# Attention in 64-row and 64x64 tiles of TensorE, with the keys split 64+8 a head

## The chip, the cores and the metric

One core of a Trainium2 chip runs the kernel. The metric is the device time of one execution in microseconds, as the median of the runs whose state is fast. A ratio is the mean time of one kernel's fast runs over that of the other's fast runs of the same rounds on the same chip, so it is not quite the ratio of the medians that stand beside it. The profile is of one execution; its span is 1 to 2 us shorter than the time.

## The reference

```python
# B, H, S, D = 8, 8, 576, 64 ; pool 8, so 72 pooled keys a head
k_p = k.reshape(B, H, 72, 8, D).mean(axis=3)
v_p = v.reshape(B, H, 72, 8, D).mean(axis=3)
a   = softmax(q @ k_p^T / sqrt(D))              # B, H, 576, 72
x   = (a @ v_p) -> (4608 tokens, 512)           # heads side by side
h   = x @ w_in                                  # 512 -> 2048
out = (h - tanh(h)) @ w_out                     # 2048 -> 512
```

## The kernel before

The kernel is one software pipeline. Tokens go through the MLP in nine groups of 512; between the MLP products of group g stands the attention of batch g+1. A score slot serves two heads. Their 2 x 72 = 144 pooled keys are too many for 128 partitions, so 128 of them go in one tile and 16 are left over. The 128 keys of a pair of heads fill all rows: the keys of the one head lie in rows 0 to 63 of the contraction, those of the other in 64 to 127, with zeros between. In AV a mask on the values keeps the heads apart.

```python
def score_mms(b, t, dst, c0, c1, pairs=range(NM)):      # two products of 288 columns a slot
    for m in pairs if t == NM else (t,):
        ...
        nc.tensor.matmul(dst[p : p + w], lhsT=KB[b % 2][:, o : o + w],
                         rhs=qTs[b][:, m, c0:c1], start=True, stop=True)

def av_half(b, blk, half, x_sb, alloc):                 # three products of 130 columns a half
    ...
    ps = alloc([128, 4, D1], FP32, "x_ps")
    for n in range(3):
        nc.tensor.matmul(..., lhsT=E[:, t, c0 : c0 + 128], rhs=vb[:, s0 : s0 + 2, :], ...)
```

All loads of batches 1 to 7 are issued by the sync engine (SP), in the order keys, values, queries. The same engine issues the stores of the output and the transposes by DMA (queries, keys, x). Each main load is one transfer of 128 rows:

```python
def load_main(src, dst, b, t0, t1):
    return nc.sync.dma_start(out=dst[:, t0:t1, :], in_=src[b, 0:128, t0:t1, :])
def load_v(b):
    return [load_main(v_pairs, v_raw[b % 2], b, 0, NM)] + load_left(v_pairs, v_raw[b % 2], b)
...
for g in range(1, NG):                                  # the loop over token groups
    for i in range(NHID):
        mlp_h(g, i, gts)
        if i == 0 and g > 1:
            pool_k(nb, nc.gpsimd); pool_v(nb, nc.gpsimd)
        if i == (3 if g == 1 else 8):
            k_dma_transpose(nb); k_place(nb, nc.gpsimd.tensor_copy)
            load_k(nb + 1); load_v(nb + 1); load_q(nb + 1)
```

The softmax here doesn't subtract the row's maximum and nothing guards it: scores larger than these inputs give would overflow.

Of the kernel before, what the change touches and what calls it, by code (L numbers as in the profile page):

```python
# [31 lines left out]
KP = 160  # L32
# [5 lines left out]
def kernel(  # L38
# [19 lines left out]
    ps_h = ctx.enter_context(tc.tile_pool(name="ps_h", bufs=3, space=PSUM))  # L58
    ps_o = ctx.enter_context(tc.tile_pool(name="ps_o", bufs=2, space=PSUM))
    ps_a = ctx.enter_context(tc.tile_pool(name="ps_a", bufs=3, space=PSUM))  # L60
# [14 lines left out]
    spread = const.tile([128, 128], BF16, name="spread")  # L75
    mask = const.tile([128, 3 * NM, 1], FP32, name="mask")
    k_raw = [const.tile([128, NT, POOL * D], FP32, name=f"k_raw{i}") for i in range(2)]
    v_raw = [const.tile([128, NT, POOL * D], FP32, name=f"v_raw{i}") for i in range(2)]
    KB = [const.tile([128, NM * KP], BF16, name=f"KB{i}") for i in range(2)]
    q_bf = const.tile([128, R + 1, H, D], BF16, name="q_bf")  # L80
    warm = const.tile([128, 1], FP32, name="warm")
    VB = [const.tile([128, 3 * NM, D1], BF16, name=f"VB{i}") for i in range(2)]
# [18 lines left out]
    def load_main(src, dst, b, t0, t1):  # L101
        return nc.sync.dma_start(out=dst[:, t0:t1, :], in_=src[b, 0:128, t0:t1, :])

    def load_left(src, dst, b, eng=nc.sync):
        return [
            eng.dma_start(out=dst[32 * t : 32 * t + LO, NM, :], in_=src[b, 128:PR, t, :])
            for t in range(NM)
        ]

    def load_dense(src, dst, b, eng=nc.sync):  # L110
        return eng.dma_start(
            out=dst[0 : NM * LO, NM, :], in_=src[b, 128:PR, :, :]
        )

    def load_k(b):
        return [
            load_main(k_pairs, k_raw[b % 2], b, 0, NM),
            load_dense(k_pairs, k_raw[b % 2], b),
        ]

    def load_v(b):
        return [load_main(v_pairs, v_raw[b % 2], b, 0, NM)] + load_left(
            v_pairs, v_raw[b % 2], b
        )
# [67 lines left out]
    def pool_k(b, eng, t0=0, t1=NT, mid=()):  # L192
        r = k_raw[b % 2].rearrange("p t (j d) -> p t j d", d=D)[:, t0:t1, :, :]
        if b not in kdups:
            kdups[b] = work.tile([128, NT, 2, D], BF16, name="kd", tag="kd")
        kd = kdups[b][:, t0:t1, :, :]
        n = t1 - t0
        first = eng.tensor_tensor(  # L198
            out=r[:, :, 0:4, :], in0=r[:, :, 0:4, :], in1=r[:, :, 4:8, :], op=ALU.add
        )  # L200
        for c in mid:
            load_w2(c)
        eng.tensor_tensor(  # L203
            out=r[:, :, 0:2, :], in0=r[:, :, 0:2, :], in1=r[:, :, 2:4, :], op=ALU.add
        )
        eng.tensor_tensor(  # L206
            out=kd,
            in0=r[:, :, 0:1, :].to_broadcast([128, n, 2, D]),
            in1=r[:, :, 1:2, :].to_broadcast([128, n, 2, D]),
            op=ALU.add,  # L210
        )
        return first

    def pool_v(b, eng):
# [8 lines left out]
            out=r[:, :, 0, :], in0=r[:, :, 0, :], in1=r[:, :, 1, :], op=ALU.add  # L223
        )
        v_main(VB[b % 2], r[:, :, 0:1, :], eng, 0, NM)
        v_left(VB[b % 2], r[:, NM, 0:1, :], eng)

    def v_main(vb, vs, eng, t0, t1):
        n = t1 - t0
        eng.tensor_tensor(  # L230
            out=vb[:, 2 * t0 : 2 * t1, 0:D].rearrange("p (t s) d -> p t s d", s=2),
            in0=vs[:, t0:t1, :, :].to_broadcast([128, n, 2, D]),
            in1=mask[:, 2 * t0 : 2 * t1, :]
            .rearrange("p (t s) o -> p t s o", s=2)
            .to_broadcast([128, n, 2, D]),
# [3 lines left out]
    def v_left(vb, vs, eng):  # L239
        eng.tensor_tensor(  # L240
            out=vb[:, 2 * NM :, 0:D],
            in0=vs.to_broadcast([128, NM, D]),
            in1=mask[:, 2 * NM :, :].to_broadcast([128, NM, D]),
            op=ALU.mult,
        )

    def kb_main(kb, ps, t0, t1, engs):
        kv = kb.rearrange("p (t x) -> p t x", x=KP)
        engs[0](out=kv[0:D, t0:t1, 0:G], in_=ps[0:D, :, 0:G])
        engs[1](out=kv[D:128, t0:t1, G:128], in_=ps[D:128, :, G:128])  # L250

    def kb_left(kb, ps, eng):
        eng(
            out=kb[D:128, :].rearrange("p (t x) -> p t x", x=KP)[:, :, 128 : 128 + LO],
            in_=ps[D:128, 0 : NM * LO].rearrange("p (x t) -> p t x", t=NM),
        )
# [10 lines left out]
    def k_transpose(b, alloc, engs=(nc.vector.tensor_copy, nc.scalar.copy)):  # L267
        kd = kdups.pop(b)
        ps = alloc([128, NM, 128], FP32, "kT_ps")
        for t in range(NM):  # L270
            turn_tile(ps[:, t, :], kd, t)
        kb_main(KB[b % 2], ps, 0, NM, engs)
        ps = alloc([128, 128], FP32, "kT_ps")
        turn_tile(ps[:, :], kd, NM)
        kb_left(KB[b % 2], ps, nc.vector.tensor_copy)

    kTs = {}

    def k_dma_transpose(b):
        kT = work.tile([128, NT, 128], BF16, name="kT", tag="kT", bufs=1)  # L280
        nc.sync.dma_start_transpose(
            out=kT[:, :, :], in_=kdups.pop(b)[:, :, :, :].rearrange("p t a d -> p (t a d)")
        )
        kTs[b] = kT

    def k_place(b, eng):
        kT = kTs.pop(b)
        kb_main(KB[b % 2], kT[:, 0:NM, :], 0, NM, (eng, eng))
        kb_left(KB[b % 2], kT[:, NM, :], eng)

    E_tiles = {}

    def score_mms(b, t, dst, c0, c1, pairs=range(NM)):
        for m in pairs if t == NM else (t,):
            o = m * KP + (128 if t == NM else 0)
            w = 32 if t == NM else 128
            p = 32 * m if t == NM else 0
            nc.tensor.matmul(  # L298
                dst[p : p + w],
                lhsT=KB[b % 2][:, o : o + w],  # L300
# [5 lines left out]
    def scores(b, t):  # L306
        if t == 0:
            E_tiles[b] = work.tile([128, NT, S], BF16, name="E", tag="E")
        E = E_tiles[b]
        hs = S // 2  # L310
        pss = []
        for half in range(2):
            ps = ps_a.tile([128, hs], FP32, name="s_ps", tag="ps_a")
            score_mms(b, t, ps[:, :], half * hs, (half + 1) * hs)
            pss.append(ps)
        for half, ps in enumerate(pss):
            nc.scalar.activation(  # L317
                out=E[:, t, half * hs : (half + 1) * hs], in_=ps[:, :], func=ACT.Exp, scale=SCALE
            )

    def scores_wide(b, ts):
        if b not in E_tiles:
            E_tiles[b] = work.tile([128, NT, S], BF16, name="E", tag="E")
        E = E_tiles[b]
        for t in ts:
            ps = ps_any([128, QA], FP32, "s_ps")
            score_mms(b, t, ps[:, :], 0, QA)
            nc.scalar.activation(out=E[:, t, 0:QA], in_=ps[:, :], func=ACT.Exp, scale=SCALE)

    def scores_tail(b):  # L330
        ps = ps_any([128, NT, QT], FP32, "s_ps")
        for t in range(NT):
            score_mms(b, t, ps[:, t, :], QA, S)
        nc.scalar.activation(
            out=E_tiles[b][:, :, QA:S], in_=ps[:, :, :], func=ACT.Exp, scale=SCALE
        )

    def av_half(b, blk, half, x_sb, alloc):
        E = E_tiles[b]
        vb = VB[b % 2]  # L340
        c0 = blk * 128 if blk < 4 else S - 128
        ps = alloc([128, 4, D1], FP32, "x_ps")
        for n in range(3):
            t = 2 * half + n if n < 2 else NM
            s0 = 2 * t if n < 2 else 2 * NM + 2 * half
            nc.tensor.matmul(  # L346
                ps[:, 2 * n : 2 * n + 2, :].rearrange("p h d -> p (h d)")
                if n < 2
                else ps.rearrange("p (a s) d -> p a s d", s=2)[:, :, 1, :],
                lhsT=E[:, t, c0 : c0 + 128],  # L350
                rhs=vb[:, s0 : s0 + 2, :].rearrange("p h d -> p (h d)")
                if n < 2
                else vb[:, s0 : s0 + 2, :],
                start=(n == 0),
                stop=(n == 2),
                skip_group_check=True,
            )
        rden = work.tile([128, 4, 1], FP32, name="rden", tag="rden", bufs=4)
        nc.vector.reciprocal(out=rden[:, :, :], in_=ps[:, :, D:D1])  # L359
        nc.vector.tensor_tensor(  # L360
            out=x_sb[:, half, :, :],
            in0=ps[:, :, 0:D],
            in1=rden[:, :, :].to_broadcast([128, 4, D]),
            op=ALU.mult,
        )

    def new_x():
        return work.tile([128, 2, 4, D], BF16, name="x_sb", tag="x_sb", bufs=4)

    def av(b, blk, alloc, by_dma):  # L370
        x_sb = new_x()
        for half in range(2):
            av_half(b, blk, half, x_sb, alloc)
        if by_dma:
# [4 lines left out]
                in_=x_sb[p0:128, :, :, :].rearrange("p a h d -> p (a h d)"),  # L379
# [3 lines left out]
    def x_pe_transpose(b, blk, x_sb, fbs=(0, 4)):  # L383
        p0 = 0 if blk < 4 else 64
        pos = b * S + blk * 128
        f0, f1 = fbs
        xf = x_sb.rearrange("p a h d -> p (a h d)")
# [417 lines left out]
```

## Time and profile before

| | before |
|---|---|
| time, median of fast runs | 301.04 us (300.99 to 301.22) |
| span of the profile | 299.1 us |
| TensorE busy, granted clock | 97%, 1.00 |
| one undisturbed token group with attention | 30.81 us |
| first tanh (the start is over) | 21.9 us |

The group times in this document are the distances between the first tanh of one token group and that of the next, read from ScalarE's rows in the trace. The chain (the work that ended last, followed back from each piece to what released it) is shown in the prediction. What matters for the argument and is not shown there is how the sync engine issues the loads of one batch. This is its time line in the kernel before (start in us, length in us, engine and line, operation, target and source, number of instructions):

```profile
126.53 0.57 SPq L102 DMA_DIRECT2D k_raw<-in_k_dram  x1
127.16 0.63 SPq L111 DMA_DIRECT2D k_raw<-in_k_dram  x1
127.84 0.58 SPq L102 DMA_DIRECT2D v_raw<-in_v_dram  x1
128.46 1.93 SPq L106 DMA_DIRECT2D v_raw<-in_v_dram  x4
130.44 0.42 SPq L135 DMA_DIRECT2D q_raw<-in_q_dram  x1
132.17 0.67 SPq L127 DMA_DIRECT2D q_raw<-in_q_dram  x1
```

An issue here takes about half a microsecond of the engine, for 1 MB (0.57 and 0.58) as for the small left-over transfers (0.63, and 1.93 for four), and the whole batch is issued in 6.3 us. After that the queue is free for stores and transposes.

### The profile page before, as it was taken

To read this page: it belongs to the slowest core of one execution; us is meant where nothing else is said; L and a number is where in the kernel's file an instruction comes from. 1 tells how busy PE (TensorE), PEld (TensorE's weight loads), DVE (VectorE), ACT (ScalarE), POOL (GpSimd) and SP (SyncE) were. 2 spreads that over 40 slices of the span, in tenths; PEclk is the share of its full clock that TensorE was granted. 3 is DMA by queue.
4 is the path that set the end of the run, shared out by engine and by line. 5 is a ranking of instruction groups with operands and counts; after the bars stand their busy time and mean duration, and the time that the engine had idled before them with its cause. 6 is when DMAs were issued, how large, how long until landed. Compare 5 with 4: busy or idle time off the path is not lost.

```text
span 299.1 us, 4694 instructions
## 1 busy us (share of the span) xinstructions
PE 291.5 (97%) x1671; PEld 142.5 (48%) x1671; DVE 159.1 (53%) x343; ACT 149.4 (50%) x283; POOL 115.5 (39%) x110
## 2 busy tenths in 40 slices
PE   7989999999999999999999999999999999999994
PEld 3454455544544454445444554455445544444443
DVE  5658665673547444753476247716680758108600
ACT  4647583666146633654265516650665166126511
POOL 8500904871496109922971089307940000000000
PEclk9999999999999999999999999999999999999999
DMA  7999999849854998699648974897431430111032
GB/s 251 226 211 278 311 227 310 263 87 328 234 113 99 271 297 134 117 302 245 107 88 235 300 167 94 242 294 159 97 66 35 95 92 0 37 70 36 0 72 70
DMA packets 66183, 49.79 MB, mean 166 GB/s; under 512 B 39920, under 2 KB 52976, under 8 KB 66160
## 3 DMA queue, kind: packets, MB, share of 16 engines
q1 hardware_dynamic: 58832, 42.94, 56.0%
q0 software_dynamic: 4752, 4.72, 9.4%
q10 hardware_dynamic: 2576, 1.84, 2.3%
q8 instruction: 13, 0.21, 0.3%
q14 instruction: 10, 0.08, 0.1%
HBM read 36.70 MB, written 9.44 MB: 154 GB/s over the span
## 4 chain that ended last, share of the span: by engine, by line
PE 85%; DMA 9%; POOL 4%; issue 0%; SPq 0%; ACT 0%; DVE 0%; POOLq 0%
PE o_ps L456 40%; PE hT_ps L428 37%; DMA w1b<-in_moe_w_in_dram 4%; PE x_ps L346 4%; DMA k_raw<-in_k_dram 4%; PE s_ps L298 3%; POOL k_raw L198 1%; DMA out_dram<-o_sb 1%; POOL k_raw L203 1%; POOL kd L206 1%; POOL w2b L510 0%; PE xT_ps L390 0%; POOL v_raw L576 0%; PE qT_ps L171 0%; POOL w1b L503 0%
## 5 line engine op out<-in xcount | busy, mean ns | idle before, releaser
L456 PE MATMUL o_ps<-w2b,gT 128*128 128x512 bf16 x560 | 134.4, 380 | 0.0
L441 DVE TENSOR_TENSOR gT<-hT_ps,t_sb 128x512 bf16<-128x512 f32 x144 | 98.9, 691 | 57.7 <-ACT t_sb L439 57.6
L428 PE MATMUL hT_ps<-xT,w1b 128*128 128x512 bf16 x576 | 126.9, 379 | 0.3 <-ACT xT L397 0.3
L439 ACT ACTIVATE t_sb<-hT_ps 128x512 f32<-128x512 f32 x144 | 85.6, 597 | 38.3 <-PE hT_ps L428 37.5
L428 PEld LDWEIGHTS <-w1b 128*128 128x128 bf16 x576 | 55.9, 98 | 66.5 <-issue 0.4
L456 PEld LDWEIGHTS <-gT 128*128 128x128 bf16 x560 | 52.5, 98 | 52.0 <-issue 1.4
L465 ACT COPY o_sb<-o_ps 128x512 f32<-128x512 f32 x33 | 19.3, 585 | 75.2 <-PE o_ps L456 75.2
L359 DVE RECIPROCAL rden<-x_ps 128x4 f32<-128x4 f32 x80 | 14.2, 177 | 52.5 <-PE x_ps L346 52.0
L360 DVE TENSOR_TENSOR x_sb<-x_ps,rden 128x256 bf16<-128x256 f32 x80 | 34.0, 425 | 3.5 <-DMA xT<-x_sb 0.6
L148 POOL CAST q_bf<-q_raw 128x2048 bf16<-128x2048 f32 x6 | 11.3, 1888 | 59.9 <-issue 34.8
L198 POOL TENSOR_TENSOR k_raw<-k_raw 128x1280 f32<-128x1280 f32 x7 | 20.2, 2886 | 27.4 <-DMA k_raw<-in_k_dram 16.6
L317 ACT ACTIVATE E<-s_ps 128x288 bf16<-128x288 f32 x60 | 21.4, 410 | 13.2 <-PE s_ps L298 13.0
L346 PE MATMUL x_ps<-VB,E 128*128 128x130 bf16 x240 | 20.8, 221 | 0.4 <-ACT xT L397 0.3
L346 PEld LDWEIGHTS <-E 128*128 128x128 bf16 x240 | 16.9, 98 | 8.8 <-DVE VB L230 0.6
L216 POOL TENSOR_TENSOR v_raw<-v_raw 128x1280 f32<-128x1280 f32 x6 | 17.4, 2898 | 0.0
L298 PE MATMUL s_ps<-qT,KB 128*128 128x288 bf16 (+5 forms) x128 | 17.0, 290 | 0.2
L298 PEld LDWEIGHTS <-KB 128*128 128x128 bf16 (+1 forms) x128 | 7.0, 96 | 10.2 <-issue 3.5
L527 PE MATMUL warm_ps<-xT 128*128 128x512 bf16 x29 | 10.2, 465 | 1.3 <-DVE xT L539 1.3
L206 POOL TENSOR_TENSOR kd<-k_raw 128x640 bf16<-128x640 f32 x7 | 10.8, 1540 | 0.5
L203 POOL TENSOR_TENSOR k_raw<-k_raw 128x640 f32<-128x640 f32 x7 | 10.8, 1541 | 0.5
L397 ACT CAST xT<-xT_ps 128x256 bf16<-128x256 f32 (+1 forms) x14 | 5.8, 436 | 8.5 <-PE xT_ps L390 5.1
L219 POOL TENSOR_TENSOR v_raw<-v_raw 128x640 f32<-128x640 f32 x6 | 9.3, 1544 | 0.5
(73 smaller groups left out, 100.7 us busy)
## 6 DMA issues: line engine op xcount, KB each, us to landing
k_raw<-in_k_dram SPq DMA_DIRECT2D x7, 1024.0 KB, 5.9
q_raw<-in_q_dram SPq DMA_DIRECT2D x7, 1024.0 KB, 10.2
v_raw<-in_v_dram SPq DMA_DIRECT2D x7, 1024.0 KB, 9.3
out_dram<-o_sb SPq DMA_DIRECT2D x38, 128.0 KB, 2.4
out_dram<-o_sb SPq DMA_DIRECT2D x16, 256.0 KB, 3.7
w1b<-in_moe_w_in_dram POOLq DMA_DIRECT2D x4, 512.0 KB, 14.2
w2b<-in_moe_w_out_dram POOLq DMA_DIRECT2D x4, 512.0 KB, 16.9
k_raw<-in_k_dram SPq DMA_DIRECT2D x7, 128.0 KB, 5.8
```

The source lines that it names most:

```text
L198: first = eng.tensor_tensor(out=r[:, :, 0:4, :], in0=r[:, :, 0:4, :], in1=r[:, :, 4:8, :], op=ALU.add)
L216: eng.tensor_tensor(out=r[:, :, 0:4, :], in0=r[:, :, 0:4, :], in1=r[:, :, 4:8, :], op=ALU.add)
L298: nc.tensor.matmul(dst[p : p + w], lhsT=KB[b % 2][:, o : o + w], rhs=qTs[b][:, m, c0:c1], start=True, stop=True,)
L317: nc.scalar.activation(out=E[:, t, half * hs : (half + 1) * hs], in_=ps[:, :], func=ACT.Exp, scale=SCALE)
L346: nc.tensor.matmul(ps[:, 2 * n : 2 * n + 2, :].rearrange("p h d -> p (h d)") if n < 2 else ps.rearrange("p (a s) d -> p a s d", s=2)[:, :, ...
L359: nc.vector.reciprocal(out=rden[:, :, :], in_=ps[:, :, D:D1])
L360: nc.vector.tensor_tensor(out=x_sb[:, half, :, :], in0=ps[:, :, 0:D], in1=rden[:, :, :].to_broadcast([128, 4, D]), op=ALU.mult,)
L428: nc.tensor.matmul(h_tiles[i][:, :], lhsT=w1b[:, fb, i * 128 : (i + 1) * 128], rhs=xT[:, fb, tok0 : tok0 + TG], start=(fb == 0), stop=(fb ...
L439: nc.scalar.activation(out=t_sb[:, :], in_=h_ps[:, :], func=ACT.Tanh)
L441: nc.vector.tensor_sub(out=gT[:, :], in0=h_ps[:, :], in1=t_sb[:, :])
L456: nc.tensor.matmul(o_ps[:, :], lhsT=gts[i][:, tb * 128 : (tb + 1) * 128], rhs=w2b[:, i, :], start=(i == 0), stop=(i == NHID - 1),)
L465: (nc.vector.tensor_copy if g == 0 and tb % 2 else nc.scalar.copy)(out=o_sb[:, :], in_=o_ps[:, :])
```

## The change

The intent is to use the array for four heads at once. A score slot becomes four products in 64x64 tiles (two row halves by two column halves), and AV becomes pairs of products in tiles of 64 rows, one head in each, so that masks on keys and values fall away. For that, the 72 keys of a head are split into 64 in the main tile and 8 left over. Batch 0 gets AV into two PSUM banks at once, with one pass of VectorE over both. For the row halves the values have to lie head by head, and so they are loaded otherwise:

```diff
-def load_main(src, dst, b, t0, t1):
-    return nc.sync.dma_start(out=dst[:, t0:t1, :], in_=src[b, 0:128, t0:t1, :])
+def load_main(src, dst, b, ts):
+    return nc.sync.dma_start(out=dst[:, ts, :], in_=src[b, LH : LH + 128, ts, :])
+def v_rows_of(b, t):
+    r0 = G * t + (LH if t % 2 == 0 else 0)
+    return v_rows[b].rearrange("(i r) n -> i r n", i=2)[:, r0 : r0 + 64, :]
 def load_left(src, dst, b, eng=nc.sync):
-    return [eng.dma_start(out=dst[32 * t : 32 * t + LO, NM, :], in_=src[b, 128:PR, t, :])
-            for t in range(NM)]
+    return [eng.dma_start(out=dst[2 * i :: 4, NM, :], in_=left_rows(src, b, i)) for i in range(2)]
+def load_v_main(b):
+    return [nc.sync.dma_start(out=v_raw[b % 2][:, t, :], in_=v_rows_of(b, t)) for t in range(NM)]
 ...
+def score_main(b, j, dst, c0, c1):
+    for s, i in ((0, 0), (1, 1), (0, 1), (1, 0)):
+        m = j + 2 * i
+        nc.tensor.matmul(dst[s][64 * i : 64 * i + 64],
+            lhsT=kTs[b][64 * s : 64 * s + 64, m, 64 * s : 64 * s + 64],
+            rhs=qTs[b][64 * s : 64 * s + 64, m, c0:c1], start=True, stop=True)
 ...
+def av_mms(b, blk, pss):               # eight products of 65 columns, two of 260, in row halves
+    mms = [(pss[i][:, t, :], i, t, vb[64 * i : 64 * i + 64, t, :])
+           for t in range(NM) for i in range(2)] + [...]
 ...   (PSUM as one tile with fixed banks; batch 0: av_blk over two banks; masks, spread gone)
```

## The prediction

> **What bounds the kernel now.** I read the page first, then the chain of work that ended last, then single stretches of the time line.
>
> ```profile
> PE 291.5 (97%) x1671; PEld 142.5 (48%) x1671; DVE 159.1 (53%) x343; ACT 149.4 (50%) x283; POOL 115.5 (39%) x110
> ...
> L456 PE MATMUL o_ps<-w2b,gT 128*128 128x512 bf16 x560 | 134.4, 380 | 0.0
> ...
> L428 PE MATMUL hT_ps<-xT,w1b 128*128 128x512 bf16 x576 | 126.9, 379 | 0.3 <-ACT xT L397 0.3
> ```
>
> TensorE is busy for 97% of the 299.1 us, and no other engine above 53%. The two MLP products hold 261 us of it and the change does not touch them. What can move is the attention work between them and the start. One batch of the steady loop, in the chain of work that ended last (start, length, what):
>
> ```profile
> 99.76 1.73 PE o_ps L456 x8
> 101.49 0.25 PE s_ps L298 x2
> 101.73 0.86 PE o_ps L456 x4
> ...
> 105.92 0.36 PE s_ps L298 x8
> 106.28 1.83 PE o_ps L456 x8
> 108.11 0.35 PE x_ps L346 x6
> ...
> 114.16 2.59 PE o_ps L456 x12
> 116.75 13.81 PE hT_ps L428 x64
> ```
>
> The chain is TensorE alone. From one block of 64 hT products (85.95) to the next (116.75) is 30.80 us: 128 products of 512 columns at 0.216 us (13.81/64) are 27.6, so attention costs 3.2 us a batch: four score slots at 0.25, the slot of left-over keys, and five AV slots at 0.35. Only these 3.2 us can be won or lost in the six batches of the loop. The slot of left-over keys is the one place where the old kernel uses smaller tiles of the array (128*32), and its neighbourhood says what that costs:
>
> ```profile
> 74.30 0.81 PE L456 MATMUL o_ps<-w2b,gT 128*128 128x512 bf16 x3
> 75.04 0.43 PE L298 MATMUL s_ps<-qT,KB 128*32 128x288 bf16 x8
> 75.41 1.90 PE L456 MATMUL o_ps<-w2b,gT 128*128 128x512 bf16 x8
> 77.14 0.51 PE L346 MATMUL x_ps<-VB,E 128*128 128x130 bf16 x6
> ```
>
> Three o_ps products from 74.30 should end their stream at 74.95 (3 x 0.216); the small tiles start at 75.04, so 0.09 us went into entering the mode. Eight of them take 75.04 to 75.41, 0.37 us. A 288-column product costs 0.1225 (0.245/2, the ordinary slot), so eight one after another would be 0.98: they ran four at a time, 2 x 0.1225 = 0.245, and 0.12 is left for leaving the mode. The next eight products take 1.737, another 0.01. One visit to a tile mode costs about 0.22 us.
>
> In the start, the chain runs through a load and GpSimd, not TensorE:
>
> ```profile
> 5.86 12.86 DMA w1b<-in_moe_w_in_dram
> ...
> 19.21 10.84 DMA k_raw<-in_k_dram
> ...
> 30.21 2.90 POOL k_raw L198
> ...
> 36.23 1.55 POOL kd L206
> ...
> 37.82 0.45 PE kT_ps L259 x5
> ```
>
> The keys of batch 1 load only after the second piece of w1 landed, GpSimd pools them, and TensorE waits for kd at 37.82. Its previous product started at 36.925 and streamed until 37.14, so it idles about 0.7 us already: whatever TensorE finishes earlier before that point only lengthens this wait.
>
> **What the Trainium skill says.** "TensorEngine Tiling (Array Packing)", Key Properties: changing the tiling mode, not just the tile, drains TensorE. The trace agrees, at 0.22 us a visit. The same page, Gotcha 1: row tiles have to write to different PSUM banks; the diff obeys this with one bank for each row half, and no run yet shows it. "TensorE: Matmul & The Clock Gate", Part 3: Packing small matmuls: different tiles run at once, starting some 4 ns apart; the groups of four above agree. "DMA: Bandwidth & Descriptors", Why a DMA increments its semaphore by 16 and not by 1: the number of DMA engines of a transfer is the largest k up to 16 that divides the slowest dimension of both sides, and a hardware-queue transfer takes the lowest-numbered k. No load of the old kernel has a slowest dimension under 16, so its trace cannot show this. The new loads have one.
>
> **The change part by part.**
>
> Scores. Old: two products of 288 columns a slot, 0.245. New: four 64x64 tiles at once, 0.1225 + 0.01 for their starts, plus a mode visit of 0.09 + 0.12, about 0.34. So the slot gets 0.095 longer although its stream is halved, because it stands alone between 128*128 products. 4 slots x 6 batches x 0.095 = +2.3 us. Batch 1 (512 columns): two quads of 0.216 plus two visits are 0.86, four old products 0.86: nothing. The left-over slot keeps its form. Tails: two visits become chained ones, under 0.1 in all.
>
> AV. Old: six products of 130 columns, 0.35. New: eight of 65 columns and two of 260, in 64-row pairs. A 64-column product with its weight load costs 0.03 (four qt_ps products take 0.12 in the chain). If the pairs run at once: 4 x 0.03 + 0.11 (260 columns) + 0.22 = 0.45, +0.10. If the loads of the two row halves go one after another: 8 x 0.03 + 0.11 + 0.22 = 0.57, +0.22. Over 35 slots (batches 1 to 7): +3.5 or +7.7 us. I hold pairs at once likelier (two in three), as the old quads' weight loads started 3 ns apart.
>
> PSUM banks. Both banks of an AV slot are now needed at its start. DVE needs about 0.55 us a half (reciprocals start at 15.56, 16.11 and 16.65). In the loop the next slot comes 0.86 us later and needs one used bank: enough. In batch 1 a transpose takes one of the three banks too, so the second half must be done: 0.3 + 1.15 us of DVE against some 1.3 us; three slots wait about 0.15: +0.4.
>
> Start. DVE bounds batch 0's AV: eight times 0.18 + 0.42 is 4.8 us. Two banks at once make it four times 0.18 + 0.69 (the cost of a 128x512 pass, the gT row), 3.5 us: 1.3 us saved, and the spread matrix and masks go. But all that lies ahead of the wait at 37.82: worth 0.
>
> GpSimd and DVE lose the mask products (1.05 us a batch), the second key copies (1.0) and parts of the rest; with 39% and 53% busy off the chain this is worth 0.
>
> Sum of the arithmetic on TensorE: 301.0 + 2.3 + 3.5 + 0.4 = 307.2, or 311.4 with serial AV loads. The whole stream saved (0.48 + 0.55 us a batch) is less than nine mode visits of 0.22.
>
> Loads. Values came in one transfer of 128 rows by four; now come four transfers whose source counts 2 segments, then 64 rows. By the skill's rule k is 2. On the hardware queue that is the same two engines four times: 4 x 64 rows of 2 KB = 256 packets each, where it was 32. In 67 to 72 us, with loads running, the stretch view shows what a packet costs:
>
> ```profile
> 67.00:72.00 5.00, 5.00 (x27) 2.45 (x25) 2.77 (x4) 2.55 (x6) 0.97 (x3) 1.00 1.00 303
> ...
> 85.95:116.75 30.80, 30.80 (x175) 15.07 (x174) 16.68 (x36) 15.36 (x30) 13.73 (x12) 1.00 0.86 202
> ```
>
> 303 GB/s over 16 engines at share 1.00 is 18.9 GB/s each, 0.108 us a packet of 2 KB, so 256 take about 28 us (an estimate; 19 if a lone pair runs half again as fast). The engines are taken for 0.86 x 30.8 = 26 us of a period, of which the values' own 32 packets are 3.5. On the two chosen ones 23 + 19 to 28 exceeds the period of 30.8; overlapped packets count twice in a share, so I put their real need at 36 to 40 us. The x transposes, which the next group's first products need, go through the same queue behind them. That is +6 us or so in the five periods that load a further batch, and some 6 more in batches 1 and 2: about +36, on top of mode visits that partly hide in the new waits.
>
> **The rivals.** (1) Mode visits beat the saved stream and loads stay hidden: 307, or 311. For it: the 0.22 us above, and TensorE with no slack. (2) Loads on two engines become the bound: 325 to 350. For it: the rule; against it: nothing in the trace shows the rule at k below 16, the queues may order the dimensions otherwise, and a version with carefully placed batch-0 work looks like one that had a working loop. I give it 0.4. (3) 64-row tiles enter and leave more cheaply than 128*32 (half the rows to drain): at 0.1 us a visit the 9 visits a batch cost 0.9 against 1.03 saved, and the time is 300 to 302; below that it is faster, at best 301 - 7 = 294 with free visits. I give it 0.15. (4) The start's gain survives because the keys of batch 1 come earlier (fewer bytes in the hardware queues): at most 1.3 us; the gate on w1 and 10.84 us of shared load speak against it.
>
> **Range and chances.** With 0.15 for cheap visits (near 301), 0.45 for 304 to 312, and 0.4 for 325 to 350, the median lies at the top of the middle group: 310. The lower tenth falls at about 299, the upper near 343. Faster by over 2% (under 295) needs nearly free visits: 0.07. Within 2% (up to 307): cheap visits and a good half of the middle group's lower part, 0.30. Slower: 0.63.
>
> **What would show it.** In the new chain, a score slot of four products in about 0.13 us with some 0.2 us of idle or stretched time around it, and an AV slot of 0.45 in place of 0.35; the period between hT blocks 31.5 to 31.9 us with loads hidden, or 36 and more with waits of hT products for the x transposes and values landing 20 us or more after issue (9.3 before) if rival 2 holds. In the start, kT's products should still begin near 37.8, with a longer idle before them. I am wrong if the slots come out shorter than 0.25 and 0.35, if TensorE's stream before 37 us sets the end after all, or if the values' landing stays under 12 us, which clears the loads.

## The result, and the profile after

The changed kernel takes 430.15 us (median of 4 fast runs, 428.75 to 430.35), against 301.04 us. The ratio is 1.428 (95% interval 1.425 to 1.431). That is far outside the predicted range. The page of the changed kernel says:

```profile
PE 313.7 (73%) x1881; PEld 137.1 (32%) x1916; DVE 157.1 (37%) x334; ACT 149.3 (35%) x281; POOL 108.0 (25%) x99
...
PE   7799800993491299907995499709991699999996
...
GB/s 226 181 239 169 123 99 88 49 151 140 160 51 147 151 104 134 73 178 122 167 51 170 133 142 92 138 139 124 141 54 197 115 62 61 94 0 75 25 25 75
...
SPq 32%; DMA 27%; PE 26%; POOL 10%; issue 4%; DVE 1%; POOLq 0%; ACT 0%; DVEq 0%; ACTq 0%
...
L470 PE MATMUL PS<-xT,w1b 128*128 128x512 bf16 (+1 forms) x586 | 137.9, 395 | 67.6 <-DMA xT<-x_sb 66.8
```

TensorE has a hole in every period (the slices with 0 to 5). The bytes moved are the same as before (49.77 MB against 49.79 MB), at less speed. The chain that ended last was 85% TensorE before; now it is a third SPq, the sequencer of the sync engine, and a quarter DMA. TensorE's own wait is in the row of the first MLP product: it waited 66.8 us in total for the transposes of x.

The views of waits name what came late (us in total, times, longest):

```profile
POOL q_bf L178 <- DMA q_raw<-in_q_dram: 145.3, 5, 31.9
...
DVE x_sb L412 <- DMA xT<-x_sb: 76.1, 5, 18.5
```

Neither waits for the values, whose loads were changed. They wait for queries and x transposes, whose form is as before. The time line of the sync engine shows why:

```profile
205.38 0.57 SPq L126 DMA_DIRECT2D k_raw<-in_k_dram  x1
206.01 1.25 SPq L134 DMA_DIRECT2D k_raw<-in_k_dram  x2
207.31 11.49 SPq L152 DMA_DIRECT2D v_raw<-in_v_dram  x4
218.84 5.81 SPq L134 DMA_DIRECT2D v_raw<-in_v_dram  x2
224.70 0.45 SPq L165 DMA_DIRECT2D q_raw<-in_q_dram  x1
225.19 6.78 SPq L157 DMA_DIRECT2D q_raw<-in_q_dram  x1
232.08 2.67 SPq L512 DMA_DIRECT2D out_dram<-o_sb  x3
234.85 5.83 SPq L421 DMA_TRANSPOSE xT<-x_sb  x4
```

The four value issues take 11.49 us where one took 0.58, and the batch is issued in 26.6 us instead of 6.3. While they run, the stretch view of 212 to 222 us (length; busy time of PE, PEld, DVE, ACT and POOL with counts; clock, DMA share, GB/s) reads:

```profile
212.00:222.00 10.00, 9.84 (x78) 3.73 (x77) 1.89 (x6) 5.03 (x13) 0.00 (x0) 1.00 0.13 49
```

A share of 0.13 is two engines of sixteen (0.125), and 49 GB/s is 24.5 GB/s for each. A value transfer has 256 KB, so at 49 GB/s it takes 5.3 us. The third and fourth value issues take 4.62 and 5.22 us in the chain. So once a few such transfers are under way, an issue lasts about as long as one of them. It is the engine that is held, whatever it issues next: the first left-over transfer behind them, of 64 KB only, takes 5.22 us to issue too, and the 128 KB tail of the queries 6.78. Stores, queries and transposes of x stand behind it.

How this becomes a period of 47 us is seen in the chain, from one issue of the loads (205.38) to the next (252.48):

```profile
213.58 5.22 SPq L152
...
218.84 5.22 SPq L134
...
224.70 13.38 DMA q_raw<-in_q_dram
...
238.14 0.59 POOL q_bf L178
...
246.61 2.91 POOL v_raw L246
...
249.60 1.54 POOL v_raw L249
```

The sync engine needs 19.3 us to get to the queries (205.38 to 224.70), these need 13.4 us to land, GpSimd then needs 13.0 us for casting them and pooling keys and values, which it does in order (238.14 to 251.14), and the transpose of the keys takes 1.3 us more (251.16 to 252.43) before the next loads may be issued. That is 47.0 us, and the gaps between make it 47.1. It is a loop of work each piece of which waits for the piece before, and no part of it is TensorE.

The last batch, for which nothing more is loaded, shows what the tiles alone do:

```profile
351.62 0.25 PE PS L320 x4
351.86 0.97 PE PS L499 x4
...
358.68 0.34 PE PS L393 x10
359.02 0.97 PE PS L499 x4
```

L320 is the score slot, L393 AV, L499 the second MLP product. A score slot takes 0.25 us of chain as before, and the four products after it 0.97 us where they took 0.86; so 0.11 us of leaving the mode is charged to them. AV takes 0.34 + 0.97 in place of 0.35 + 0.86.

The start is later too. These are links of the chain:

```profile
8.56 15.70 DMA w1b<-in_moe_w_in_dram
...
24.28 9.65 DMA k_raw<-in_k_dram
...
39.39 8.40 SPq L152
...
47.84 22.82 DMA v_raw<-in_v_dram
```

The second piece of w1 lands at 24.26 us in place of 18.72. GpSimd now issues six value loads for batch 0 ahead of w1, so this piece is issued at 8.56 in place of 5.86, and it takes 15.70 us in place of 12.86 to land. The values of batch 1 land at 70.7 us; VectorE waits for them, and then TensorE for VectorE.

With the start of each group the whole difference is placed (us; "start" is the first tanh):

| kernel | start | group 0 | 1 | 2 | 3 | 4 | 5 | 6 | 7 |
|---|---|---|---|---|---|---|---|---|---|
| before | 21.9 | 34.14 | 30.81 | 30.80 | 30.81 | 30.81 | 30.81 | 30.81 | 27.63 |
| after | 28.0 | 57.57 | 63.32 | 47.91 | 46.12 | 47.07 | 46.51 | 32.24 | 27.63 |

Of the 127.9 us between the spans, 6.1 are in the start, 23.4 and 32.5 in the first two groups, 64.4 in the next four (groups 1 to 5 each load a further batch), and 1.4 in the last with attention.

### The profile page after: what moved, and what is told of

It reads as the page before. It is cut to its first block, busy times and chain, and to the rows that moved or that the text cites. A ratio compares the mean times of both kernels' runs of the same rounds, so it can differ in the third digit from the quotient of the medians.

```text
span 427.0 us, 5172 instructions
## 1 busy us (share of the span) xinstructions
PE 313.7 (73%) x1881; PEld 137.1 (32%) x1916; DVE 157.1 (37%) x334; ACT 149.3 (35%) x281; POOL 108.0 (25%) x99
## 2 busy tenths in 40 slices
DMA packets 69529, 49.77 MB, mean 117 GB/s; under 512 B 43264, under 2 KB 56384, under 8 KB 69504
## 4 chain that ended last, share of the span: by engine, by line
SPq 32%; DMA 27%; PE 26%; POOL 10%; issue 4%; DVE 1%; POOLq 0%; ACT 0%; DVEq 0%; ACTq 0%
SPq L152 17%; PE PS L470 13%; DMA q_raw<-in_q_dram 12%; PE PS L499 11%; SPq L134 8%; DMA v_raw<-in_v_dram 5%; DMA w1b<-in_moe_w_in_dram 4%; POOL v_raw L246 3%; SPq L157 2%; DMA k_raw<-in_k_dram 2%; DMA xT<-x_sb 2%; POOL k_raw L228 2%; POOL v_raw L249 2%; SPq L512 2%; PE PS L393 1%
## 5 line engine op out<-in xcount | busy, mean ns | idle before, releaser
L470 PE MATMUL PS<-xT,w1b 128*128 128x512 bf16 (+1 forms) x586 | 137.9, 395 | 67.6 <-DMA xT<-x_sb 66.8
L499 PE MATMUL PS<-w2b,gT 128*128 128x512 bf16 x537 | 133.7, 385 | 2.5 <-issue 2.1
L482 ACT ACTIVATE t_sb<-PS 128x512 f32<-128x512 f32 x144 | 85.9, 599 | 117.6 <-PE PS L470 115.4
L484 DVE TENSOR_TENSOR gT<-PS,t_sb 128x512 bf16<-128x512 f32 x144 | 99.0, 691 | 60.3 <-ACT t_sb L482 60.0
L499 PEld LDWEIGHTS <-gT 128*128 128x128 bf16 x560 | 49.5, 99 | 60.4 <-issue 4.8
L412 DVE TENSOR_TENSOR x_sb<-PS,rden 128x256 bf16<-128x256 f32 x72 | 30.6, 425 | 78.4 <-DMA xT<-x_sb 76.1
L508 ACT COPY o_sb<-PS 128x512 f32<-128x512 f32 x33 | 19.3, 586 | 78.8 <-PE PS L499 78.8
L339 ACT ACTIVATE E<-PS 128x288 bf16<-128x288 f32 (+3 forms) x74 | 27.8, 429 | 32.4 <-PE PS L320 27.9
L411 DVE RECIPROCAL rden<-PS 128x4 f32<-128x4 f32 x72 | 12.8, 177 | 71.4 <-PE PS L393 69.6
L393 PE MATMUL PS<-VB,E 64*128 64x65 bf16 x320 | 12.9, 201 | 19.3 <-DVE VB L252 19.3
L393 PEld LDWEIGHTS <-E 64*128 64x128 bf16 x400 | 9.3, 99 | 35.6 <-DVE VB L252 19.8
L320 PE MATMUL PS<-qT,kT 64*64 64x288 bf16 (+2 forms) x128 | 10.8, 321 | 12.1 <-DMA kT<-kd 12.0
L320 PEld LDWEIGHTS <-kT 64*64 64x64 bf16 x128 | 3.7, 105 | 25.0 <-DMA kT<-kd 12.5
L568 PE MATMUL PS<-xT 128*128 128x512 bf16 x28 | 10.7, 500 | 1.4 <-DVE xT L580 1.2
L393 PE MATMUL PS<-VL,E 64*128 64x260 bf16 x80 | 11.6, 285 | 0.2 <-DVE VL L261 0.2
## 6 DMA issues: line engine op xcount, KB each, us to landing
w1b<-in_moe_w_in_dram POOLq DMA_DIRECT2D x4, 512.0 KB, 13.4
```

The lines of the kernel that those rows point to most:

```text
L339: nc.scalar.activation(out=out, in_=in_, func=ACT.Exp, scale=SCALE)
L393: nc.tensor.matmul(dst, lhsT=E[64 * i : 64 * i + 64, t, c0 : c0 + 128], rhs=rhs, start=(n < 2), stop=(n >= len(mms) - 2), skip_group_check ...
L412: nc.vector.tensor_tensor(out=x_sb[:, i, :, :], in0=ps[:, :, 0:D], in1=rden[:, :, :].to_broadcast([128, NM, D]), op=ALU.mult,)
L470: nc.tensor.matmul(h_tiles[i][:, c0:c1], lhsT=w1b[:, fb, i * 128 : (i + 1) * 128], rhs=xT[:, fb, tok0 + c0 : tok0 + c1], start=(fb == 0 an ...
L482: nc.scalar.activation(out=t_sb[:, :], in_=h_ps[:, :], func=ACT.Tanh)
L484: nc.vector.tensor_sub(out=gT[:, :], in0=h_ps[:, :], in1=t_sb[:, :])
```

## The experiments

Theory A: the loads over few DMA engines hold the sync engine, the loop closes through whatever stands behind them in its queue, and TensorE's tiles cost only what the prediction worked out, some 0.9 us a group (4 x 0.095 + 5 x 0.10). Rival B: it is throughput, two engines simply have more to move than fits into a period. Rival C: the PE part (visits, banks, later AV) makes the new waits, and the loads only follow. (The expectations give the letters to other rivals in places; each says what it means by them.) The twelve runs:

| run | kernel | time us | ratio to before (95%) | output |
|---|---|---|---|---|
| e1_v64 | after, values over 16 engines | 321.19 | 1.067 (1.065 to 1.070) | correct |
| e2_left8 | e1, left-over rows over 8 engines | 340.82 | 1.131 (1.126 to 1.135) | correct |
| e3_q_first | after, queries issued ahead of values | 428.46 | 1.423 (1.419 to 1.426) | correct |
| e4_before_v2 | before, values over 2 engines | 418.15 | 1.388 (1.384 to 1.392) | wrong |
| e5_before_v4 | before, values over 4 engines | 349.62 | 1.160 (1.157 to 1.164) | wrong |
| e11_before_v8 | before, values over 8 engines | 317.54 | 1.054 (1.048 to 1.060) | wrong |
| e6_left16 | e1, left-over rows over 16 engines | 310.30 | 1.029 (1.025 to 1.032) | wrong |
| e7_before_left4 | before, new left-over loads only | 303.33 | 1.006 (1.003 to 1.010) | wrong |
| e8_grouped | e1, fewer visits to tile modes | 320.27 | 1.061 (1.057 to 1.065) | correct |
| e9_repaired | e1, all loads over 16 engines | 319.68 | 1.061 (1.055 to 1.067) | correct |
| e10_repaired_grouped | e9 with fewer visits | 316.26 | 1.050 (1.046 to 1.054) | correct |
| e12_left16_grouped | e6 with fewer visits | 304.14 | 1.012 (1.009 to 1.016) | wrong |

"Wrong" means that rows of another head are loaded; sizes, types and all arithmetic stay. Their group times:

| run | start | group 0 | 1 | 2 | 3 | 4 | 5 | 6 | 7 |
|---|---|---|---|---|---|---|---|---|---|
| e1_v64 | 24.8 | 36.59 | 36.64 | 33.44 | 31.76 | 33.02 | 31.75 | 31.76 | 27.63 |
| e2_left8 | 28.4 | 37.00 | 42.18 | 35.73 | 33.31 | 39.02 | 33.42 | 31.75 | 27.63 |
| e3_q_first | 28.3 | 60.05 | 58.29 | 48.89 | 46.50 | 46.75 | 46.74 | 32.82 | 27.63 |
| e4_before_v2 | 22.1 | 60.71 | 58.32 | 47.03 | 45.39 | 46.63 | 46.01 | 31.73 | 27.63 |
| e5_before_v4 | 22.1 | 50.32 | 38.21 | 38.50 | 35.88 | 38.35 | 35.58 | 30.81 | 27.63 |
| e11_before_v8 | 22.1 | 39.57 | 32.85 | 36.42 | 32.18 | 34.09 | 30.81 | 30.81 | 27.63 |
| e6_left16 | 22.7 | 35.24 | 34.41 | 31.76 | 31.76 | 31.76 | 31.76 | 31.76 | 27.63 |
| e7_before_left4 | 21.8 | 37.74 | 30.81 | 30.81 | 30.81 | 30.81 | 30.81 | 30.81 | 27.63 |
| e8_grouped | 23.4 | 40.42 | 36.56 | 32.80 | 31.74 | 32.37 | 32.47 | 30.55 | 27.58 |
| e9_repaired | 27.0 | 34.44 | 37.37 | 33.76 | 31.76 | 31.76 | 31.75 | 31.76 | 27.63 |
| e10_repaired_grouped | 26.9 | 34.43 | 36.14 | 32.24 | 32.34 | 31.33 | 31.70 | 30.55 | 27.58 |
| e12_left16_grouped | 24.9 | 34.44 | 31.47 | 30.59 | 30.55 | 30.55 | 30.55 | 30.55 | 27.58 |

### Values over sixteen engines (e1_v64)

```diff
-    nc.sync.dma_start(out=v_raw[b % 2][:, t, :], in_=v_rows_of(b, t)) for t in range(NM)
+    # [64 rows, 2 of the four head pairs, 512]: the slowest dimension is 64, four transfers as before
+    nc.sync.dma_start(out=dst[64 * i : 64 * i + 64, j:NM:2, :], in_=src[i, r0 : r0 + 64, :, :])
```

> The changed kernel with the same four value transfers a batch, cut so that their slowest dimension is 64 rows (one row half, two heads' blocks) and not 2. Theory A (the values run on two DMA engines, and everything behind them on the sync queue waits): the 2-engine stretches of 49 GB/s vanish, the period of the loop falls from 47.1 to 31.5-32.0 us, the time to 307-311 us, that is what the mode visits of TensorE cost (+0.95 us a batch in the undisturbed last batch of the changed kernel). Rival B (the four-engine transfers of left-over rows, or the larger number of transfers, bind as well): the time stays above 315 us with waits for loads. Rival C (the new tile forms themselves stall TensorE): above 330 us.

It took 321.19 us. So 109 of the 129 us go with the form of four transfers a batch (those of batch 0, which GpSimd issues, included): same bytes, same number of issues, same products on TensorE. Rival C is out as the main cause. The figure that was expected is missed by 10 us at its upper end, and what came is the other case that the expectation names (above 315 us, with waits for loads). The table says where: the undisturbed groups are at 31.76, but the start and the groups 0, 1, 2 and 4 are longer. The two left-over loads of values and of keys still have four as their slowest dimension. The next runs ask whether it is they.

### Two engines in the old kernel (e4_before_v2)

```diff
-def load_v(b): return [load_main(v_pairs, v_raw[b % 2], b, 0, NM)] + load_left(...)
+def load_v(b): return load_v_main(b) + load_left(...)   # 2 segments x 64 rows, as in the change
```

> The old kernel, its attention untouched, with the values of batches 1 to 7 loaded by four transfers of 2 segments by 64 rows as in the changed kernel (rows wrong on purpose, so the result is wrong; times are what counts). Theory A: this alone makes the old kernel slow, to 400-430 us (batch 0's values stay on 16 engines, so some 6 us less than the changed kernel's start). Rival C (the slowdown needs the new tiles or the new layout): under 330 us.

418.15 us. The old kernel, with its scores, AV, banks and batch 0 untouched, loses 117 us by the value loads of batches 1 to 7 alone, and its groups are those of the changed kernel to within some 5 us (group 1), mostly within 1. The sync engine again:

```profile
198.75 11.62 SPq L127 DMA_DIRECT2D v_raw<-in_v_dram  x4
210.41 7.23 SPq L106 DMA_DIRECT2D v_raw<-in_v_dram  x4
```

The second row is the old kernel's left-over loads. Behind its own single value load they took 1.93 us for four; here they take 7.23, standing behind the slow ones.

### Queries ahead of the values (e3_q_first)

```diff
-load_v(nb + 1)
-load_q(nb + 1)
+load_q(nb + 1)
+load_v(nb + 1)
```

> The changed kernel with its two-engine value transfers, but the queries of the next batch are issued ahead of the values. Theory A1 (the period of 47 us is a loop: queries wait behind the values on the queue, GpSimd waits for the queries and pools the keys after them, the next loads are issued after the keys' transpose): the loop opens, the period falls to what the two engines need, 36-40 us as I predicted, the time to 350-385 us. Rival A2 (47 us is the two engines' own need): no change, 425-435 us.

428.46 us, no gain, in the range that A2 gives. My first form of theory A, in which the late queries alone closed the loop, falls. The chain of this run shows the second way round:

```profile
221.86 3.70 SPq L134
...
225.61 2.72 SPq L134
...
230.40 2.60 SPq L421
...
233.09 7.00 DMA xT<-x_sb
...
240.14 7.94 PE PS L470 x24
```

The queries are now issued at 206.2, but the transposes of x (L421) still come after the value loads; they are issued at 230.4 and land at 240.1, and only then can TensorE begin the group's products, after whose first ones the next loads are issued (250.96). From 204.32 to 250.96 is 46.6 us, the same period by another path. So in this run, too, what the period waits for stands behind the value loads in the queue. A2, the two engines' own need, would give the same figure; the next runs ask about it.

### Four and eight engines (e5_before_v4, e11_before_v8)

```diff
-rearrange("(i r) n -> i r n", i=2)[:, r0 : r0 + 64, :]
+rearrange("(i r) n -> i r n", i=4)[:, r0 : r0 + 32, :]      # e11: i=8, 16 rows
```

> As e4_before_v2 (old kernel, wrong rows), but each value transfer has 4 segments of 32 rows, so by the rule it runs on four engines. Theory A (a loop through the one queue: the loads, the x transposes behind them and the next loads follow one another, so that a period is the larger of 30.8 us and about 25 us plus the time of the value transfers, 21 us on two engines): on four engines 10.5 us, period near 36 us, time 328-345 us. Rival (the two engines' own throughput sets the 46 us, no loop): on four engines they need under 30 us a period, so the loop is back at 30.8 us and the time at 301-312 us.

> As e4_before_v2 and e5_before_v4, with 8 segments of 16 rows, so eight engines by the rule: the value transfers need about 5.2 us a batch. Loop theory (period = larger of 30.8 us and some 25 us plus the values' time; 46.2 us on two engines, 35.6-38.5 on four): 30.8 us or up to 32, time 301-312 us.

Four engines: 349.62 us, with groups of 35.6 to 38.5. The sync engine's issues are shorter, as they should be if a held issue lasts as long as the transfer:

```profile
197.22 3.63 SPq L127 DMA_DIRECT2D v_raw<-in_v_dram  x4
200.89 4.24 SPq L106 DMA_DIRECT2D v_raw<-in_v_dram  x4
```

Issuing a batch takes 15.2 us (195.91 to 211.05), 9 less than with two engines in the same kernel (197.45 to 221.37 is 23.9), and the loop shrinks by about as much, from 46 to 37. This speaks against a mere limit of throughput (rival B). An estimate: four engines at 24.5 GB/s move the 1 MB of values in 10.7 us, a third of a period. Even with all of the 23 us of other traffic that the prediction counts, that is 33.7 us, and the groups take 35.6 to 38.5. The margin is small, and for two engines the same sum (23 + 21.4 = 44.4) is not far from the 46 measured. But the trace of the changed kernel agrees that the engines have slack: in the 14.3 us from the landing of the queries to the next loads (238.14 to 252.48) there are 3.7 us, counted over the packets of its trace, in which no transfer at all is in flight, while GpSimd works. So B does not hold alone; how much it adds to the loop was not separated. The figure expected of e5 is passed by some 5 us at its upper end, through group 0 with 50.32.

Eight engines: 317.54 us, 5 us above the upper end of what was expected. From group 5 on its groups are undisturbed (30.81). Groups 0, 2 and 4 are still longer. Here the four value issues take 2.61 us, no longer than ordinary ones, so the hold on the sync engine is gone and something smaller is left, argued and not tested: with three more loads a batch and slower ones, queries and values still land later, and GpSimd's chain of casts and poolings with them. I have not separated these.

### The left-over rows (e2_left8, e6_left16, e7_before_left4)

```diff
 # e2: eight transfers of 8 rows in place of two whose slowest dimension is 4
+out=dst[2 * i + 32 * t : 2 * i + 32 * t + 29 : 4, NM, :], in_=left_rows(src, b, i)[t, :, :]
 # e6: two transfers of 32 rows (other rows than wanted, same bytes)
+return src[b, 32 * i : 32 * i + 32, 0, :]
 # e7: the kernel before, with the left-over loads of the change and nothing else of it
```

> As e1_v64, and the left-over rows of keys and values in eight transfers of 8 rows (slowest dimension 8) in place of two with slowest dimension 4. Theory A: nothing is left to win from loads, within 1% of e1_v64, if anything slower by the six further issues per load at 0.5 us each on the sync queue. Rival B (four engines still bind): faster than e1_v64 by over 3 us.

> As e1_v64, with the left-over rows of keys and values taken from 32 neighbouring rows each (wrong rows on purpose, result wrong), so that these transfers too run on 16 engines; their number stays. If the stalls that e1_v64 has beyond TensorE's own 31.76 us (its groups of 36.6, 33.4, 33.0 us) come from the four-engine transfers, the time falls to 308-313 us and every group after the first two is within 0.3 us of 31.8. If they come from the number and order of the transfers, it stays at 318-322 us.

> The old kernel with only the left-over rows of keys and values loaded as in the changed one (two transfers each with slowest dimension 4; placed wrongly, result wrong). If four-engine transfers of 64 KB each cost what e1_v64 lost beyond TensorE: 306-312 us. If they are hidden here, 300-303 us.

e2 was meant as the repair, expected within 1% of e1, and made it worse, 340.82 us. Eight engines in place of four did not pay for four times as many issues:

```profile
118.07 5.43 SPq L137 DMA_DIRECT2D k_raw<-in_k_dram  x8
```

against 1.25 us for two in e1. Values and keys together have 16 such issues a batch, about 0.7 us each. This fits theory A, with the sync engine's time spent on many quick issues in place of few slow ones, but it is not shown apart: e2 also gives GpSimd six more loads at the start (first tanh at 28.4 in place of 24.8).

e6, with as few issues as e1 and sixteen engines, came out as expected: 310.30 us, and from group 2 on every group is 31.76. So the remaining holes of e1 in the loop come from the four-engine left-over loads. That leaves 0.95 us a group over the 30.81 of before, with the chain on TensorE alone; e8 asks whether it is the mode visits. e7 shows that these left-over loads cost the old kernel only 2 to 3 us, in group 0 (37.74 against 34.14); in the changed kernel they cost 11 (e1 against e6).

### Fewer visits to the tile modes (e8_grouped)

```diff
-if 1 <= u <= NT: scores(nb, u - 1)
-if u in (7, 8, 9, 10, 12): av(...)
+for n in {2: (0, 1), 4: (2, 3, 4)}.get(u, ()): scores(nb, n)
+for blk in {8: (0, 1, 2), 12: (3, 4)}.get(u, ()): av(nb, blk, ps_c1, True)
+ps_c = Banks(5, 6, 7, 0, 1, 2)
```

> e1_v64 with the same products in fewer visits to the tile modes in the loop: two score slots together, the other two with the left-over keys, AV blocks 0 to 2 together and 3 and 4, in the six PSUM banks that are free then. Theory (0.22 us per visit, 10 visits become 4 and one change between tile modes at about 0.1): an undisturbed group falls from 31.76 to about 30.5 us, below the old kernel's 30.80; the time falls by 5-7 us against e1_v64 if the load stalls stay as they are. Rival (the slots themselves are longer, not the visits): group 31.5-31.8 us. Second rival (bunched work makes VectorE or the x transposes late): groups over 31 us with waits of hT products.

The last group with attention, which no load disturbs, takes 30.55 us against 31.76: 1.21 us for five visits fewer (the nine that the change added become four), 0.24 each, close to the 0.22 of the prediction. A little of it may belong to the left-over slot, which has a mode of its own and now follows one of them directly (counted as a sixth visit saved, it makes 0.20 each). The whole time, 320.27 us, is hardly better than that of e1, where 5 to 7 us were expected: the loads still stall the other groups, and joining AV slots brings a stall of its own, as the expectation's second rival had it. This chain runs up to that last group:

```profile
220.85 6.64 DMA xT<-x_sb
...
227.57 0.42 DVE x_sb L415
...
228.12 0.43 DVE x_sb L415
...
228.60 1.67 PE PS L473 x7
```

With three AV slots at once VectorE runs out of its four x buffers: it waits until a transpose of x has landed, and TensorE waits for what VectorE then hands on.

### The repair (e9_repaired, e10_repaired_grouped) and its limit (e12_left16_grouped)

```diff
 # e9: the left-over keys of a pair of heads are the rows 64 to 79 of its 144, so that every load
 #     has a slowest dimension of 16 or 64; main keys and values are then rows 0..63 and 80..143
-return nc.sync.dma_start(out=dst[:, ts, :], in_=src[b, LH : LH + 128, ts, :])
+return [nc.sync.dma_start(out=dst[p : p + 64, ts, :], in_=src[b, r : r + 64, ts, :])
+        for p, r in ((0, 0), (64, PR - 64))]
+after(load_v_main(1), w1_dmas[3])
 # e10: e9 + the joined slots of e8 + eight buffers of x in place of four
 # e12: e6 + joined slots, AV two steps earlier {7: (0, 1, 2), 10: (3, 4)} + eight buffers of x
```

> The changed kernel with its tiles as they are and a key split whose loads all have a slowest dimension of 16 or 64 (main keys are the first 64 of the even head and the last 64 of the odd one, so the left-over rows of a pair are 16 neighbours); values of batch 1 issued only after the last piece of w1. Correct result. What then is left is TensorE: every group from the third on at 31.76 us as in e6_left16, the first two within 2 us of the old kernel's 34.1 and 30.8 plus 0.9: time 306-310 us. If load stalls remain (13 transfers a batch in place of 9): over 312 us.

> e9_repaired with the grouped slots of e8_grouped (4 visits to tile modes a batch in place of 10) and eight x buffers in place of four. Groups at 30.5-30.6 us as in the last undisturbed group of e8_grouped, against 30.81 of the old kernel; time 299-302 us: level with the old kernel, at best 0.6% under it. If bunched AV makes the x transposes late: groups of 31 us and more, time over 303 us.

> The changed kernel with the value loads and the left-over loads over 16 engines (wrong left-over rows on purpose, as in the run that measured 310.3), and the attention slots of the loop joined: scores 0 and 1 in one visit, 2, 3 and the left-over slot in a second, AV blocks 0, 1, 2 in a third and 3, 4 in a fourth, AV two steps earlier than in the earlier joined runs so that the x transposes have time, and eight x buffers. Theory (visits to the tile modes are all that is left of the cost once loads are hidden): the undisturbed group takes 30.55 us as the last one of the earlier joined run, 1.2 less than 31.76, in the five groups from the third on, and the time is 310.3 - 6 = 302 to 305, within 2% of the kernel before. Rival (joining the slots makes a new wait, for the x transposes or for PSUM): groups of 31.2 or more with TensorE waiting in them, 306 to 310. Neither theory expects a time under 299.

e9 and e10 are correct kernels with no load under sixteen engines, and they missed what was expected by 10 and 14 us (319.68 and 316.26). For e9 the expectation named this case (over 312 us if 13 transfers a batch in place of 9 still stall), for e10 too (over 303). In the loop e9 is what it should be, 31.76 from group 3 on. It loses in two other places. Its first tanh is at 27.0 us: GpSimd issues eight loads for batch 0 ahead of w1 and begins w1 at 9.73 us, where the kernel before began at 5.12. Groups 0 to 2 are longer than in the kernel before by 0.3, 6.6 and 3.0 us. And e10's joined slots keep a stall even with eight x buffers, as its chain shows at the end of one group:

```profile
215.35 0.39 PE PS L398 x10
...
218.04 5.89 DMA xT<-x_sb
...
223.98 1.04 PE PS L475 x4
```

The chain goes from the joined visit of three AV slots (L398) through their normalisations on VectorE, one after another, to the transposes of x, issued at 218.04 behind loads and stores. TensorE works meanwhile and then waits 0.97 us for them. Group 6, for which no loads are issued, has no such stall (30.55). e12 places AV two steps earlier and has the loads of e6; which of the two takes the stall away is not separated. Its chain in the loop is again TensorE alone:

```profile
106.30 0.37 PE PS L322 x8
...
111.92 0.82 PE PS L395 x30
...
115.44 0.58 PE PS L395 x20
```

Three AV slots in one visit take 0.82 us (0.27 each), two take 0.58. All groups from 2 on are 30.55 to 30.59 us. That is up to 0.26 us less than before, 1.3 us in all groups from 2 on, and the start (24.9 against 21.9; in e6, whose start is the same code, it was 22.7) and groups 0 and 1 (0.3 and 0.7) take more than that back. The time is 304.14 us and the ratio 1.012, which counts as the same. So even with its loads out of the way, and with wrong rows to get there, the change does not win; no version beat the kernel before.

## Why the prediction was wrong

It named the cause as its second rival and gave it 0.4, with 325 to 350 us; the time is 430. By its steps:

**The rule for the number of engines** held as it had been taken from the skill ("DMA: Bandwidth & Descriptors", Why a DMA increments its semaphore by 16 and not by 1): a share of 0.13 and 49 GB/s on the new loads. The first of the three doubts that kept the weight at 0.4 was "nothing in the trace shows the rule at k below 16", and it was too large a doubt. The signs that the prediction listed for this rival are those that came: periods over 36 us, and products that wait for the x transposes.

**The size of the load step failed.** "I put their real need at 36 to 40 us … That is +6 us or so in the five periods … and some 6 more in batches 1 and 2: about +36." This treats the two engines as a pipe and compares its fill with the period. The estimate of a lone pair (19 us for a batch's values) was close: the issues of values and left-over rows took 17.3 us (11.49 + 5.81), and 1 MB at 49 GB/s is 21 us. What was missing is that the sync engine does not stay free meanwhile. Its issue of a two-engine transfer lasted 5.22 us, as long as the transfer, so the slow loads added about 20 us of serial time (26.6 against 6.3) to a queue that the queries, stores and x transposes share. The prediction did see the x transposes "behind them" in that queue, and drew no number from it. What each slow period cost was 15.3 to 17.1 us in four of the five groups that load a further batch, in place of 6, and 32.5 in the fifth (group 1) and 23.4 in group 0, in place of 12 together. e4 shows the loads alone (+117 us), e3 that issuing the queries first does not help, e5 that the period shrinks with the issue time. That the hold, and not the throughput of the two engines, makes most of it rests on the time lines and on e5.

**The arithmetic on TensorE** was right, and it is the part that hardly counted. Predicted was a period of 31.5 to 31.9 with loads hidden, measured 31.76 in e6; 0.095 us more for a score slot against 0.11, and 0.10 for an AV slot against 0.10. That AV pairs run at once (the likelier of the two readings) held: a slot is 0.34 us and 0.11 on the products after it, 0.45 in all, the figure for pairs, where serial loads were put at 0.57. e6, with its loads hidden, is at 310.30, where 307.2 was worked out; its groups 0 and 1 are 1.1 and 3.6 us longer, of which the 0.4 for PSUM banks is at most a part.

**Rival 3** (cheaper visits) is refuted by 0.24 us a visit in e8 against 0.1. **Rival 4 and the start**: "worth 0" was optimistic. The passes of AV in batch 0 did get closer together (from 14.61 to 19.03 us before its last slot begins, now from 20.64 to 23.03), but they begin 6 us later. The values of batch 0 come in six transfers of another form from GpSimd's queue, and w1 stands behind them; with the form of e1 alone, the start is at 24.8 in place of 28.0, so about half of the 6.1 us goes with that form. "kT's products should still begin near 37.8" failed with it: the keys of batch 1 were issued at 24.28 in place of 18.73.

**The clock** is a cost that the prediction left out. "TensorE: Matmul & The Clock Gate", Part 1, has the throttled clock after idle, and the trace agrees: 0.50 while TensorE was idle (189.0 to 194.9 us) and a mean of 0.64 over the 8.2 us after. After this hole 24 products took 8.24 us, 0.343 each in place of 0.216, which is 3 us of TensorE's time for such a stall.

**What remains open.** Why the sync engine is free for the first value issues (0.53 and 0.99 us) and is held from the third on is not told by any record; a bound on what may be outstanding would look like this, but nothing here shows it. Few engines are not the only way to it: at the start of e1 the first value issue, over sixteen engines, lasted 7.61 us (from 21.31), with the DMA share at 1.15. The stalls of the first two groups in e1, e9 and e11 were narrowed to load landings and GpSimd, not to one wait. Issuing the values from another engine's queue was not tried.

## What to carry to other kernels

When a change regroups the dimensions of a load, look at the slowest dimension of both sides first. With a few transfers over two DMA engines under way, single issues here held the engine for 5 to 7 us, so ask what else stands in that engine's queue and whether the next loads wait for it. A load's size against the period is not enough: draw the loop (issue, land, compute on it, next issue) and add its pieces. And a tile mode of the array has a fee for each visit, here some 0.2 us: with one slot a visit a group took 31.76 us, with slots joined 30.55, against 30.81 without the change.

## What the Trainium skill lacked or had wrong

- "DMA: Bandwidth & Descriptors", section Issuing engines are not separate DMA queues, calls the time that it takes to initiate a DMA "usually small relative to the DMA itself". For most transfers over sixteen engines that holds here (0.58 us). With transfers over two engines it doesn't: the third and fourth issues of a batch took 4.62 and 5.22 us, about as long as a transfer of 256 KB at 49 GB/s, and the engine issued nothing else meanwhile. No section of that page says that the issuing engine can be held so.
- The same page's rule for k gives no rate, but its Specifications give about 27 GiB/s for one DMA engine. Measured: 49 GB/s at a share of 0.13, so 24.5 GB/s an engine, with 2 KB rows.
- "TensorEngine Tiling (Array Packing)", Key Properties, says that changing the mode drains TensorE and gives no figure. Measured: 1.21 us for five visits, 0.24 us each, by e8; 0.20 to 0.21 by the time lines (0.09 in, 0.11 to 0.12 out).
